# A second pair of f tiles of the first chunk by seven products, with its first loads reordered and later chunk loads on ScalarE's queue

## The chip, the cores and the metric

The kernel runs on one core of a Trainium2 chip. The metric is the device time of one execution in microseconds (us). The recorded time before is 542.76 us, the median of three runs (542.32 to 544.04). A profile covers one execution and its span is some 1.8 us shorter than the metric (540.9 us against 542.71 in the profiled run before).

In the profile PE is TensorE's matmuls, PEld its weight loads, DVE is VectorE, ACT ScalarE, POOL GpSimd and SP SyncE; a `q` behind the name means the engine's DMA queue. A bank is one of the buffers in which TensorE adds up its results. A line of the timeline gives start, length, engine, line of the kernel, operation, output and inputs, form, count, and in brackets what ended the idle time before it.

## The reference

```python
# x: 2048 x 1024, w_gate and w_up: 1024 x 3584, w_down: 3584 x 1024, all bf16
def reference(x, w_gate, w_up, w_down):
    return (_gelu(x @ w_gate) * (x @ w_up)) @ w_down
```

## The kernel before

The kernel works in two halves of 1024 tokens. In each, it goes through 28 tiles of 128 columns of f, for two blocks of 512 tokens. Two f tiles, two halves of the inner dimension and two token blocks make a 2 x 2 by 2 x 2 block product, which takes eight block products plainly, or seven by a Strassen-like scheme. `pair_quads` does the seven (M1 to M7). Its weights' sums (s1 to s4) and the sums of x (t1 to t4) are fp32r tiles; M1 and M2 multiply bf16 blocks as they were loaded. A chunk is the load of the gate and up weights of four f tiles, thus of two pairs. "Product" alone means VectorE's multiplication of gelu(gate) by up, into `hT`; a "bank addition" is VectorE adding the copy of M5 to a bank.

```python
        def do_m5(j):
            mm(V_[j], j, s(j, "s1"), tsum["t1"], True)
            m5[j] = m_pool.tile([P, TB], F32, name=f"m5_{j}")
            act(nc.scalar.copy(out=m5[j][:], in_=banks[V_[j]][:]))
            ...
        for j in range(2):                       # M7
            mm(RB[j], j, s(j, "s3"), tsum["t3"], False)
            add_m5(V_[j], RB[j])                 # VectorE, PSUM + SBUF
            ...
        for j in range(2):                       # M4: needs RB[j] free, and t4
            mm(RB[j], j, s(j, "a22"), tsum["t4"], False)
```

In the first half, the first chunk (four f tiles, two pairs) is done plainly, in eight units of 16 bf16 matmuls, while the sums are made beside it; pair 2 is the first by seven products:

```python
            first_units(hT)                      # tiles 0 and 1, first token block
            unit(hT, PB, 2, 0)
            t_sum("t1")
            unit(hT, QB, 3, 0)
            ...                                  # t2, b22, unit (0,1), t3, s sums of pair 2
            unit(hT, RB, 1, 1)
            t_sum("t4")
            unit(hT, QB, 2, 1)
            unit(hT, VB, 3, 1)
            first_pair = PPG                     # 2
```

In the later pairs of that half VectorE also makes sums of w_down ("steps", into `o_sb` buffers, stored to `t_dram`), and x of the second half is transposed into `o_sb` buffers and stored to `x_dram`.

## Time and profile before

| | before |
|---|---|
| time, median | 542.76 us |
| span of the profile | 540.9 us |
| PE busy, share of the span | 534.2 us, 99% |
| DVE, ACT, POOL busy | 360.4, 258.4, 246.0 us |
| first matmul of pair 2 | 34.19 us |

The table says that only fewer or quicker matmuls, or gaps of TensorE, can shorten this kernel. The lines behind it stand in the prediction. Busy time of TensorE is no pace: its matmuls overlap in the trace, so I read the distance of their starts.

### The profile page before, as it was taken

How to read it: one execution, taken by the hardware profiler on the slowest of the kernel's cores; microseconds unless marked ns; L12 is line 12 of the kernel's file. 1: busy time of each engine (PE TensorE's matmuls, PEld its weight loads, DVE VectorE, ACT ScalarE, POOL GpSimd, SP SyncE). 2: the span in 40 equal slices, each digit the busy share in tenths (PEclk: the TensorE clock that was granted, in tenths of full speed). 3: DMA queues.
4: the chain of work that ended last, by engine and by line, in shares of the span. 5: the costliest groups of instructions: out<-in, count | busy, mean ns of one | idle time of the engine just before them, and what ended most of it. 6: DMA issues, size and time to landing. Idle time of an engine off the chain costs nothing.

```text
span 540.9 us, 7082 instructions
## 1 busy us (share of the span) xinstructions
PE 534.2 (99%) x2356; PEld 374.8 (69%) x2392; DVE 360.4 (67%) x465; ACT 258.4 (48%) x439; POOL 246.0 (45%) x206
## 2 busy tenths in 40 slices
PE   8999999999999999999999999999999999999997
PEld 3457777766676676767776667777777766866865
DVE  0747878787886998889573433444445469969961
ACT  2435555555555319216465555555554552452270
POOL 0187888888887000000046777667777730000000
PEclk9999999999999999999999999999999999999999
DMA  9926495685837976779950405041331456677846
GB/s 221 307 80 209 125 341 161 211 256 191 277 132 227 333 240 219 266 248 311 331 196 1 155 2 155 4 153 42 114 98 59 155 204 209 228 242 247 288 148 205
DMA packets 84771, 102.70 MB, mean 190 GB/s; under 512 B 18688, under 2 KB 66304, under 8 KB 84736
## 3 DMA queue, kind: packets, MB, share of 16 engines
q1 hardware_dynamic: 83136, 101.47, 58.8%
q10 hardware_dynamic: 1600, 0.79, 0.6%
q8 instruction: 19, 0.31, 0.2%
q14 instruction: 16, 0.13, 0.1%
HBM read 85.98 MB, written 12.58 MB: 182 GB/s over the span
## 4 chain that ended last, share of the span: by engine, by line
PE 95%; DMA 3%; issue 1%; POOL 0%; ACTq 0%; DVE 0%; ACT 0%; SPq 0%
PE bank L388 58%; PE bank L658 32%; PE bank L252 5%; DMA x_dram<-o_sb 2%; DMA w_mem<-in_w_up_dram 1%; POOL s_mem L360 0%; ACTq L161 0%; DVE hT L276 0%; ACT o_sb L711 0%; ACTq L167 0%; SPq L161 0%; DVE o_sb L593 0%; ACTq L711 0%; SPq L612 0%
## 5 line engine op out<-in xcount | busy, mean ns | idle before, releaser
L388 PE MATMUL bank<-t_mem,s_mem 128*128 128x512 f32 x1016 | 240.4, 395 | 0.1
L388 PEld LDWEIGHTS bank<-t_mem,s_mem 128*128 128x128 f32 x1016 | 190.8, 188 | 42.5 <-DVE hT L276 0.5
L360 POOL TENSOR_TENSOR s_mem<-w_mem 128x512 fp32r<-128x512 bf16 x100 | 119.3, 1213 | 191.6 <-DVE t_mem L244 102.2
L658 PE MATMUL bank<-t_mem,s_mem 128*128 128x512 f32 x544 | 127.4, 393 | 0.0
L276 DVE TENSOR_TENSOR hT<-w_mem,bank 128x512 bf16<-128x512 f32 x104 | 70.6, 686 | 75.7 <-PE bank L388 42.5
L658 PEld LDWEIGHTS bank<-t_mem,s_mem 128*128 128x128 f32 x544 | 102.0, 188 | 22.5 <-issue 0.5
L411 DVE TENSOR_TENSOR bank<-bank,m 128x512 f32<-128x512 f32 x104 | 68.0, 694 | 56.2 <-ACT m L433 51.9
L388 PE MATMUL bank<-xT,w_mem 128*128 128x512 bf16 x391 | 93.0, 380 | 1.3
L271 ACT ACTIVATE w_mem<-bank 128x512 f32<-128x512 f32 x104 | 61.0, 596 | 62.3 <-DVE bank L411 39.0
L388 PEld LDWEIGHTS <-w_mem 128*128 128x128 bf16 x416 | 38.7, 98 | 49.8 <-issue 6.3
L360 POOL TENSOR_TENSOR s_mem<-w_mem,s_mem 128x512 fp32r<-128x512 bf16 x50 | 65.8, 1337 | 0.0
L568 DVE TENSOR_TENSOR t_mem<-w_mem 128x1024 fp32r<-128x1024 bf16 x56 | 65.6, 1218 | 0.0
L360 POOL TENSOR_TENSOR s_mem<-s_mem,w_mem 128x512 fp32r<-128x512 f32 x50 | 63.2, 1284 | 0.0
L438 ACT COPY bank<-bank 128x512 f32<-128x512 f32 x52 | 29.6, 570 | 38.2 <-PE bank L388 37.9
L373 ACT CAST s_mem<-w_mem 128x512 fp32r<-128x512 bf16 x52 | 32.0, 615 | 29.1 <-PE bank L388 25.4
L633 DVE TENSOR_TENSOR s_mem<-hT 128x512 fp32r<-128x512 bf16 x52 | 35.7, 714 | 10.2 <-PE bank L658 9.4
L658 PEld LDWEIGHTS <-hT 128*128 128x128 bf16 x224 | 21.3, 98 | 26.6 <-issue 2.1
L433 ACT COPY m<-bank 128x512 f32<-128x512 f32 x52 | 30.5, 587 | 17.4 <-PE bank L388 17.4
L442 ACT COPY bank<-bank 128x512 f32<-128x512 f32 x52 | 29.6, 570 | 13.8 <-PE bank L388 13.8
L711 ACT CAST o_sb<-bank 128x512 bf16<-128x512 f32 x28 | 15.3, 585 | 39.7 <-PE bank L658 39.7
L593 DVE TENSOR_TENSOR o_sb<-wd_sb,o_sb 128x512 fp32r<-128x512 bf16 x28 | 33.6, 1200 | 0.4
L252 PE MATMUL bank<-xT,w_mem 128*128 128x512 bf16 x125 | 28.0, 379 | 0.6 <-DMA w_mem<-in_w_up_dram 0.4
(42 smaller groups left out, 252.4 us busy)
## 6 DMA issues: line engine op xcount, KB each, us to landing
t_mem<-t_dram SPq DMA_DIRECT2D x56, 512.0 KB, 5.3
w_mem<-in_w_gate_dram SPq DMA_DIRECT2D x11, 1024.0 KB, 5.5
w_mem<-in_w_up_dram SPq DMA_DIRECT2D x11, 1024.0 KB, 7.9
wd_sb<-in_w_down_dram SPq DMA_DIRECT2D x28, 256.0 KB, 4.4
t_dram<-o_sb SPq DMA_DIRECT2D x28, 256.0 KB, 2.4
wd_sb<-in_w_down_dram SPq DMA_DIRECT2D x12, 512.0 KB, 8.3
w_mem<-in_w_down_dram SPq DMA_DIRECT2D x10, 512.0 KB, 6.2
w_mem<-in_w_down_dram SPq DMA_DIRECT2D x4, 1024.0 KB, 6.6
```

The lines of the kernel that those rows point to most:

```text
L252: nc.tensor.matmul(ps[:], lhsT=w_sb[:, kd, fi * P : (fi + 1) * P], rhs=xT[tb][:, kd, :], start=(kd == 0), stop=(kd == KD - 1),)
L271: act(nc.scalar.activation(out=g_sb, in_=ps[:], func=ACT.Gelu_apprx_tanh))
L276: nc.vector.tensor_tensor(out=hT[:, fc, tb * TB : (tb + 1) * TB], in0=g_sb, in1=ps[:], op=ALU.mult,)
L360: pool(nc.gpsimd.tensor_tensor(out=t, in0=in0, in1=in1, op=op))
L373: act(nc.scalar.copy(out=t, in_=a(1, 1)))
L388: nc.tensor.matmul(banks[bank][:], lhsT=lhs[:, c, :], rhs=rhs[:, c, :], start=start and c == 0, stop=c == KH - 1, skip_group_check=True,)
L411: nc.vector.tensor_tensor(out=banks[dst][:], in0=banks[src][:], in1=m5[j][:], op=ALU.add)
L433: act(nc.scalar.copy(out=m5[j][:], in_=banks[V_[j]][:]))
L568: dve(nc.vector.tensor_tensor(out=t, in0=in0, in1=in1, op=ALU.subtract))
L593: dve(nc.vector.tensor_tensor(out=t, in0=in0, in1=in1, op=ALU.subtract))
L633: dve(nc.vector.tensor_tensor(out=t, in0=in0, in1=in1, op=op))
L658: nc.tensor.matmul(banks[bset[u]][:], lhsT=lhs(i, u), rhs=rhs(i), start=start and i == 0, stop=stop and i == NS - 1, skip_group_check=True,)
```

## The change

The diff is shortened; words in square brackets stand for calls. Its intent: pair 1 (f tiles 2 and 3) by seven products too; the first loads in the order in which they are needed; and the side work of the later pairs so placed that VectorE and the loads don't get in the way.

```diff
-    for j in range(2):
-        load_xT(xT, 0, 0, KH + j, KH + j + 1)
-        load_w(first, j, 2, 5, act, 0, FA)
+    load_w(first, 0, 2, 5, act, 0, FA)
+    load_w(first, 1, 2, 5, sp, 0, FA)
...
-    for j in range(2):
-        load_w(first, j, 5, KD, sp, 0, FA)
-    for kd in range(KH + 2, KD):
+    for kd in range(KH, KD):
         load_xT(xT, 0, 0, kd, kd + 1)
+        if kd == KH + 1:
+            for j in range(2):
+                load_w(first, j, 5, KD, act, 0, FA)
...
-            unit(hT, PB, 2, 0)
-            ... (six units)
+            first_pair = PPG - 1
+            for j in range(2):
+                s_sum(0, first_pair, j, "s1")              # GpSimd
+                s_sum(0, first_pair, j, "s3")
+            s_sum(0, first_pair, 0, "s2", True)            # True: on VectorE
+            s_sum(0, first_pair, 0, "s4", True)
+            t_sum("t1")
+            pair_quads(hT, 0, first_pair, (0, PPG), {}, 0) # M1 and M2 only
+            ...
+            s_sum(0, first_pair, 1, "s2", True)
+            t_sum("t2")
+            ... (tiles 0 and 1, second token block, by halves of k; t3 between)
+            s_sum(0, first_pair, 1, "s4", True)
+            t_sum("t4", 0, KH // 2)                        # other half: after M6
...
-                        load_w(key, j, 0, KD)
+                        load_w(key, j, 0, KD, act)
...
-                then["m7"] = [store_x]
-                then["m3"] = steps[:1] + [stage loads]
-                then["m4"] = steps[1:]
+                then["m2 of last"] = [chunk load] + steps[:2] + [stage_x twice]
+                then["m7"] = [store_x] + [stage loads]
+                then["m4"] = steps[2:]
```

The rest is bank numbers, the engines that copy the first transposes of x, down sums that move from M5 to M6 in pairs 7 to 10, and GpSimd's sums for pair 2, which wait for t4.

More of the change, by code (lines that the diff above doesn't have):

```diff
@@ L224, in half, with t_sum @@
         return slice(j * KH, (j + 1) * KH)
-    def t_sum(name):
+    def t_sum(name, c0=0, c1=KH):
         def b(j, l):
@@ L243, in t_sum @@
             t2 = tsum["t2"].bitcast(F32)
-            dve(tt(out=t, in0=b(1, 0), in1=t2, op=sub))
+            cs = slice(c0, c1)
+            dve(tt(out=t[:, cs], in0=b(1, 0)[:, cs], in1=t2[:, cs], op=sub))
         else:
@@ L298, in transpose_x0 @@
         for n, (kd, ts0, ts1) in enumerate(parts):
-            tp = banks[(PB + QB)[(2 * q + n) % 4]][:].bitcast(BF16)
+            tp = banks[(VB + RB[1:])[n]][:].bitcast(BF16)
             for ts in range(ts0, ts1):
@@ L308, in transpose_x0 @@
             cols = slice(ts0 * P, ts1 * P)
-            if n % 2 == 0:
+            if q == 0 or n == 0:
                 dve(nc.vector.tensor_copy(out=xT[0][:, kd, cols], in_=tp[:, cols]))
@@ L316, in first_units @@
         wg, wu = chunks[first]
-        held = (VB, RB)
+        held = (PB, RB)
         transpose_x0(0)
-        order = [(0, 0), (0, 1), (1, 0), (1, 1)]
-        order += [(j, kd) for kd in range(2, KD) for j in range(2)]
-        for j, kd in order:
+        for kd, j in [(kd, j) for kd in range(KD) for j in range(2)]:
             for u in range(2):
@@ L337, in block, with s_sum @@
         return w_sb[:, half(kh), fi * P : (fi + 1) * P]
-    def s_sum(h, pair, j, name, on_dve=False):
+    def s_sum(h, pair, j, name, on_dve=False, ring=False):
         key = (h, "p", pair)
@@ L343, in a @@
             return block(key, j, i, kh)
-        if on_dve and name in ("s1", "s2", "s3"):
+        if ring and name in ("s1", "s2", "s3"):
             if j == 0:
@@ L378, with pair_quads @@
     pending = []
-    def pair_quads(hT, h, pair, nxt, then):
+    def pair_quads(hT, h, pair, nxt, then, part=None):
         key = (h, "p", pair)
@@ L402, in prep @@
         def prep(j, name):
-            if nxt is not None:
+            if nxt is not None and part is None:
                 s_sum(nxt[0], nxt[1], j, name)
@@ L438, in do_m6 @@
             act(nc.scalar.copy(out=banks[RB[j]][:], in_=banks[QB[j]][:]))
-        for j in range(2):
-            mm(P_[j], j, block(key, j, 0, 0), b11, True)
-            act(nc.scalar.copy(out=banks[QB[j]][:], in_=banks[P_[j]][:]))
+        if part != 1:
+            for j in range(2):
+                mm(P_[j], j, block(key, j, 0, 0), b11, True)
+                act(nc.scalar.copy(out=banks[QB[j]][:], in_=banks[P_[j]][:]))
+        if part == 0:
+            m2()
+            return
         behind = len(pending) > 0
@@ L455, in pair_quads @@
         else:
-            pending.append(m2)
+            if part is None:
+                pending.append(m2)
             order = (do_m5, 0), (do_m6, 0), (do_m6, 1), (do_m5, 1)
@@ L811 @@
             first_units(hT)
-            unit(hT, PB, 2, 0)
-            t_sum("t1")
-            unit(hT, QB, 3, 0)
-            t_sum("t2")
-            t_sum("b22")
-            unit(hT, VB, 0, 1)
-            t_sum("t3")
-            for name in S_NAMES:
-                for j in range(2):
-                    s_sum(0, PPG, j, name)
-            unit(hT, RB, 1, 1)
-            t_sum("t4")
-            unit(hT, QB, 2, 1)
-            unit(hT, VB, 3, 1)
-            first_pair = PPG
+            first_pair = PPG - 1
+            for j in range(2):
+                s_sum(0, first_pair, j, "s1")
+                s_sum(0, first_pair, j, "s3")
+            s_sum(0, first_pair, 0, "s2", True)
+            s_sum(0, first_pair, 0, "s4", True)
+            t_sum("t1")
+            pair_quads(hT, 0, first_pair, (0, PPG), {}, 0)
+            for j in range(2):
+                s_sum(0, first_pair, j, "a22")
+            t_sum("b22")
+            s_sum(0, first_pair, 1, "s2", True)
+            t_sum("t2")
+            for k0 in range(0, KD, KH):
+                for u, bset in enumerate((PB, RB)):
+                    for b, w_sb in zip(bset, chunks[first]):
+                        for kd in range(k0, k0 + KH):
+                            mm_gu(banks[b], w_sb, u, 1, kd)
+                    if k0 > 0:
+                        unit_out(hT, bset, u, 1)
+                    if k0 > 0 and u == 0:
+                        t_sum("t3")
+            s_sum(0, first_pair, 1, "s4", True)
+            t_sum("t4", 0, KH // 2)
             xs = [(tb, kd) for tb in (1, 0) for kd in range(KD)]
@@ L838, in load_chunk @@
                     for j in range(2):
-                        load_w(key, j, 0, KD)
+                        load_w(key, j, 0, KD, act)
                 if key not in chunks:
                     then["m2 of last"] = [load_chunk]
-            if h == 0:
-                n = [min(4 * (pair - first_pair + d), NSTEP) for d in range(3)]
+            if h == 0 and pair >= PPG:
+                n = [min(4 * (pair - PPG + d), NSTEP) for d in range(3)]
                 steps = [lambda k=k: stage_step(k) for k in range(n[0], n[1])]
                 new = range((n[1] + 2) // 3, (n[2] + 2) // 3)
-                then["m2 of last"] = [
-                    lambda q=q: stage_x(*q) for q in xs[:2]
-                ] + then.get("m2 of last", [])
-                then["m7"] = [store_x]
-                then["m3"] = steps[:1] + [lambda i=i: stage_load(i) for i in new]
-                then["m4"] = steps[1:]
+                then["m2 of last"] = (
+                    then.get("m2 of last", [])
+                    + steps[:2]
+                    + [lambda q=q: stage_x(*q) for q in xs[:2]]
+                )
+                then["m7"] = [store_x] + [lambda i=i: stage_load(i) for i in new]
+                then["m4"] = steps[2:]
                 xs = xs[2:]
             if pair == NPAIR - 2:
-                then["m2 of last"] = [
-                    lambda: load_wd_rows(0, 4),
-                    lambda: load_wd_rows(4, 8),
-                ]
+                then.setdefault("m2 of last", []).extend(
+                    [lambda: load_wd_rows(0, 4), lambda: load_wd_rows(4, 8)]
+                )
             if 6 < pair < 11:
                 i = 2 * pair - 8
-                then.setdefault("m5", []).append(
+                then.setdefault("m6", []).append(
                     lambda i=i: s_down(hT, 0, "s3", i, i + 2)
@@ L895, with late_t4, late_s @@
                 }
-            pair_quads(
-                hT, h, pair, (h, pair + 1) if pair + 1 < NPAIR else None, then
-            )
+            if pair < PPG and h == 0:
+                def late_t4():
+                    t_sum("t4", KH // 2, KH)
+                    last_on["t4"] = last_on["dve"]
+                def late_s():
+                    last_on["pool_wait"] = last_on["t4"]
+                    for name in S_NAMES:
+                        for j in range(2):
+                            s_sum(0, PPG, j, name)
+                then = {"m5": [late_t4], "m4": [late_s]}
+            nxt = (h, pair + 1) if pair + 1 < NPAIR else None
+            part = 1 if (h, pair) == (0, PPG - 1) else None
+            pair_quads(hT, h, pair, nxt, then, part)
         then0 = {"m5": [lambda: s_down(hT, 0, "s3", 4, 6)]}
@@ L917, in s_fill @@
                 for name in names:
-                    s_sum(nh, 0, j, name, True)
+                    s_sum(nh, 0, j, name, True, True)
             then0["m6"] = [
```

## The prediction

> **What bounds the kernel now.** I read the busy shares first, then TensorE's waits, then the chain that ended last, and only then the first 35 us as a timeline, because the change rewrites just that part and reshuffles some side work of the later pairs.
>
> The busy shares and the two matmul groups that the change trades against each other:
>
> ```profile
> PE 534.2 (99%) x2356; PEld 374.8 (69%) x2392; DVE 360.4 (67%) x465; ACT 258.4 (48%) x439; POOL 246.0 (45%) x206
> ...
> L388 PE MATMUL bank<-t_mem,s_mem 128*128 128x512 f32 x1016 | 240.4, 395 | 0.1
> ...
> L388 PE MATMUL bank<-xT,w_mem 128*128 128x512 bf16 x391 | 93.0, 380 | 1.3
> ...
> L252 PE MATMUL bank<-xT,w_mem 128*128 128x512 bf16 x125 | 28.0, 379 | 0.6 <-DMA w_mem<-in_w_up_dram 0.4
> ```
>
> TensorE is busy 99% of 540.9 us and idles next to nothing before any group. The whole wait list of TensorE has two rows, both in the first 9 us:
>
> ```profile
> PE bank L203 <- PEq L962: 0.8, 1, 0.8
> PE bank L252 <- DMA w_mem<-in_w_up_dram: 0.4, 1, 0.4
> ```
>
> So time can only come from fewer or quicker matmuls, from the start, or from gaps that this wait list hides. The chain (start, length, what) shows one such gap:
>
> ```profile
> 95.68 12.51 PE bank L388 x55
> ...
> 108.24 5.94 PE bank L388 x26
> ...
> 117.29 8.13 DMA x_dram<-o_sb
> 125.48 0.57 issue
> 126.05 0.69 DVE hT L276
> 126.74 0.04 issue
> 126.79 7.12 PE bank L388 x29
> ...
> 133.96 12.52 PE bank L388 x55
> ```
>
> Pieces that begin at the same point of a pair of f tiles lie 12.56 us apart (108.24 - 95.68). From 108.24 to 133.96 there are 25.72 us instead of 25.12, so one pair lost **0.60 us**: a VectorE step waited for a store of staged x to give back its buffer, the next hT product came late behind it, and TensorE needed its bank. Everywhere else the spacing is 12.56.
>
> The start, as a timeline (start, length, engine, what, idle before it):
>
> ```profile
> 7.28 1.05 PE L252 MATMUL bank<-xT,w_mem 128*128 128x512 bf16 x4
> ...
> 8.71 25.15 PEld L252 LDWEIGHTS <-w_mem 128*128 128x128 bf16 x118 [0.87 <-DMA w_mem<-in_w_up_dram]
> 8.71 25.64 PE L252 MATMUL bank<-xT,w_mem 128*128 128x512 bf16 x115 [0.38 <-DMA w_mem<-in_w_up_dram]
> ...
> 20.67 2.18 ACT L247 CAST t_mem<-xT 128x512 fp32r<-128x512 bf16 x4 [1.23 <-DMA xT<-in_x_dram]
> ...
> 34.19 1.89 PE L388 MATMUL bank<-xT,w_mem 128*128 128x512 bf16 x8
> ```
>
> The reader is to see that from 8.71 on, TensorE runs unbroken up to the first pair by seven products at about 34.1, and that the last x of the second token block is in place only at 20.67, where ScalarE's conversion stopped waiting for it.
>
> **What the Trainium skill says.** "Perfetto Trace Analysis", section "Identifying the Most-Contended Engine", says that matmul busy time is a poor measure of headroom. This trace agrees: one matmul is listed at 380 ns, but 118 of them start over 25.64 - 0.38 = 25.26 us, thus 25.26/117 = **0.216 us** apart. "TensorE: Matmul & The Clock Gate", section "Back-to-back issue gap", gives N/2.4 + 2.5 ns for a warm matmul, 215.8 ns at N = 512; the trace has 216. No page gives the fp32r pace; I take it from the pair: 56 matmuls in 12.56 us, of which 16 bf16 take 3.45, so 40 fp32r take 9.11, or **0.228 us** each. "SBUF — State Buffer", section "Who interferes with whom", says a VectorE instruction with two SBUF inputs and a GpSimd one that reads SBUF exclude each other. The trace agrees: two GpSimd sums from 27.97 took 4.32 us together beside t3 and t4 (1.15 each alone), and t4 took 3.02 against 2.28 us for t1 to t3. "DMA: Bandwidth & Descriptors", section "Issuing engines are not separate DMA queues", says that loads issued on several engines share the same 16 DMA engines, so another queue saves issue time only. The two-microsecond windows give DMA shares of 0.98 to 1.29 from 2 to 18 us at 218 to 291 GB/s, so the start is already near what they move, and moving loads to ScalarE's queue cannot make the data come much sooner.
>
> **The change, part by part.**
> 1. *Matmuls.* Before, the first chunk is eight plain units of 16 bf16 matmuls. After, four of them (tiles 2 and 3, both token blocks, 64 matmuls, 64 x 0.216 = 13.8 us) become seven products: 16 bf16 and 40 fp32r, 12.56 us. On the path, since TensorE is the bound: **-1.25 us** (13.81 - 12.56). Seven for eight would be 12.5%, but the fp32r pace gives part of it back and one pair out of 28 is concerned.
> 2. *First loads.* The up weights of k 2 to 4 were fourth on ScalarE's queue (issued 2.38, landed 8.7) and now go out third on SyncE, at some 1.8, ahead of both x transposes. TensorE's order becomes k by k. TensorE stood without weights for 0.32 us at 7.70 and 0.87 us at 8.71. I expect the larger gap to shrink by about 0.6. The matmuls would then reach k = 4 near 9.5 instead of 10, for which the transpose, now issued half a microsecond later, is just in time. First gain, by estimate: **-0.5 us**. Ten matmuls were done at 8.71; in the new order eight should be done by about 7.8.
> 3. *New sums.* Pair 1 needs ten left sums of its own (s1 to s4 and a copy, for gate and up); those on GpSimd cost 1.15 us each, those on VectorE 0.69. They stand where GpSimd was idle (it waited 22.22 us for its first sum). VectorE has four more bank additions and the t sums must all come some 8 us sooner. Off the path if they are in time; part 4 asks.
> 4. *Deadlines.* From k = 2 at 7.8: 24 matmuls finish the first units at 13.0; M1 and M2 of pair 1 end at 16.4 (16 x 0.216); the second token block's first half is then needed, and its second half 16 matmuls later, at 19.9. Those units end at 23.3, and 40 fp32r matmuls bring the end of pair 1 to 32.4. Before, the same point was at 34.1, so the ideal gain is 1.7 us, parts 1 and 2 together. But the last x was there at 20.67 before. It goes out perhaps 1 us sooner, behind the same bytes on busy engines; I put it at 20.0 to 20.5, a wait of up to 0.5. Then VectorE has one chain from it: t2 2.28, product 0.69, t3 2.28, product 0.69, half of t4 1.14, two bank additions 1.40, the other half 1.14, one addition 0.69, together 10.3 us, ending at about 30.5 to 31, with GpSimd able to stretch a t sum by 0.7. M4 needs that bank at 30.7 in the ideal line. So I give back **+0.7 us** for x and this chain. Next, GpSimd's sums for pair 2 wait for t4: s1 twice and s2 twice are done 4 x 1.2 = 4.8 us after about 31, while M6 of pair 2 asks for s2 some 2.6 us after 33, so that is just met.
> 5. *Later pairs.* Two steps move to where the last M2 ends, chunk loads go to ScalarE, and x transposes come after them. The store that held the buffer at 117.29 is no longer behind a 2 MB chunk load on the same queue. I count most of the 0.60 us gap as gone: **-0.45 us**. ScalarE pays two issues of about 0.6 us every second pair; it has 48% load, and its next copy waits for M6 anyway, so nothing on the path.
>
> Sum: -1.25 - 0.5 + 0.7 - 0.45 = -1.5 us; 542.76 - 1.5 = 541.3 us.
>
> **The rivals.**
> (a) *The wait only moves*: the second block of x or the up weights of tiles 2 and 3 are late, because the second half of the chunk is now asked for at 13.0 (gate) and 13.9 (up) instead of 13.5 and 15.2, and the start is set by bytes. For it: the DMA shares above 1 up to 18 us, and the conversion that waited until 20.67. Against: those loads are issued a microsecond sooner. Then the start gains nothing and only the gap at 126 is saved: about 542.3 us, or 543 if GpSimd stretches the t sums too.
> (b) *Everything hidden*: the x is there by 19.9 and VectorE keeps up. Then -1.25 - 0.5 - 0.6 = -2.35, or 540.4 us.
> (c) *A new bound in the later pairs*: VectorE has two steps (0.7 to 1.3 us each) between the last M2's product and the bank additions, plus a 0.7 us down sum in pairs 7 to 10. The old trace has about 2.8 us there (112.0 to 114.83) and M3 can wait some 1 us more, so 3.4 fits, without much to spare. If it doesn't fit, each of a dozen pairs could lose 0.1 to 0.3: 543 to 544 us.
>
> **Range and chances.** Rival (b) sets the low end, 540.0 with noise; (a), or a mild (c), the high end, 542.9. The three runs before spread over 1.7 us, as much as the whole effect. A change of 2% is 10.9 us: no term here comes near, so within 2% has 0.98; I leave 0.01 for each side.
>
> **What would show it.** 64 matmuls of the plain group (L252) left instead of 128, 40 more fp32r and 16 more bf16 ones by quads; the weight wait before the third k of at most 0.3 us; the first matmul of pair 2 at about 33.1 us (34.1 before: ideal 32.4); TensorE waits between 16 and 32 us on x, on VectorE's t sums or on bank additions, together some 0.7 us; spacing of 12.56 us in all later pairs and no loss near 126. I am wrong if the pairs' spacing grows, if pair 2 starts later than 34.1, or if TensorE's wait list shows GpSimd sums.

## The result

The changed kernel takes 541.69 us (median of six runs, 541.14 to 544.24); the kernel before, run with it, 543.1 (542.32 to 544.08). The ratio is 0.9978, with a 95% interval of 0.9955 to 1.0. Ratios here are the mean time of one kernel's runs over that of the other's of the same rounds, so not quite the ratio of the medians. In a second session the changed kernel gave 541.22 (541.14 to 541.54) against 542.65, a ratio of 0.9976 [0.9961, 0.9991]. All clocks are 0.999 or 1.0. So the change brings 1.2 to 1.4 us, or 0.2%; that is far inside the 2% within which two kernels count as the same.

The page of the changed kernel, its busy shares and the same groups:

```profile
PE 534.5 (99%) x2384; PEld 377.1 (70%) x2384; DVE 362.2 (67%) x475; ACT 263.3 (49%) x446; POOL 239.5 (44%) x210
...
L389 PE MATMUL bank<-t_mem,s_mem 128*128 128x512 f32 x1056 | 249.7, 394 | 0.2 <-DVE bank L412 0.2
...
L389 PE MATMUL bank<-xT,w_mem 128*128 128x512 bf16 x432 | 98.1, 380 | 0.2 <-DMA w_mem<-in_w_up_dram 0.2
```

There are 40 more fp32r matmuls (1056 against 1016) and 16 more bf16 ones by quads (432; the weight loads before were 416), as the trade wants. TensorE now waits for VectorE's bank additions (L412) and for up weights. Three of the six rows of its wait list (waiter, waited for, us in total, times, longest; the others are 0.8 us at the very start, 0.2 for x and 0.2 for up weights):

```profile
...
PE bank L253 <- DVE xT L312: 0.2, 1, 0.2
PE bank L389 <- DVE bank L412: 0.2, 1, 0.2
PE bank L389 <- DMA w_mem<-in_w_up_dram: 0.2, 1, 0.2
...
```

The chain that ended last shows more than those small numbers. It no longer runs over TensorE in the first 32 us but over the transposed loads of x and then VectorE (start, length, what):

```profile
14.22 4.28 DMA xT<-in_x_dram
...
27.12 0.60 DVE s_mem L358
27.72 0.83 DVE t_mem L245
28.55 0.23 issue
28.78 1.28 DVE bank L412 x2
30.06 1.12 DVE t_mem L245
31.19 0.62 DVE bank L412
31.81 0.04 issue
31.85 152.82 PE bank L389 x680
```

From 31.85 us TensorE runs 152.82 us without a break, through the place near 126 us where the kernel before lost 0.60. Before 31.85, VectorE's sums and bank additions set the start of M4. The step from x to VectorE in this chain is no wait, though: VectorE was at t1 until 20.31 (17.07 + 3.24). The timeline of that start, first VectorE's, then GpSimd's and ScalarE's, then TensorE's rows:

```profile
14.69 0.91 DVE L358 TENSOR_TENSOR s_mem<-s_mem,w_mem 128x512 fp32r<-128x512 f32 x1
15.63 1.52 DVE L358 TENSOR_TENSOR s_mem<-w_mem,s_mem 128x512 fp32r<-128x512 bf16 x1
17.07 3.24 DVE L236 TENSOR_TENSOR t_mem<-xT,xT 128x2048 fp32r<-128x2048 bf16 x1
20.24 0.68 DVE L277 TENSOR_TENSOR hT<-w_mem,bank 128x512 bf16<-128x512 f32 x1
20.84 0.68 DVE L358 TENSOR_TENSOR s_mem<-s_mem,w_mem 128x512 fp32r<-128x512 f32 x1
21.44 2.28 DVE L239 TENSOR_TENSOR t_mem<-xT,t_mem 128x2048 fp32r<-128x2048 bf16 x1
...
12.78 5.38 POOL L360 TENSOR_TENSOR s_mem<-w_mem 128x512 fp32r<-128x512 bf16 x4 [11.48 <-DMA w_mem<-in_w_gate_dram]
...
18.52 2.18 ACT L248 CAST t_mem<-xT 128x512 fp32r<-128x512 bf16 x4 [0.43 <-DMA xT<-in_x_dram]
...
14.54 2.76 PE L389 MATMUL bank<-xT,w_mem 128*128 128x512 bf16 x12 [0.21 <-DMA w_mem<-in_w_up_dram]
17.14 7.07 PE L253 MATMUL bank<-xT,w_mem 128*128 128x512 bf16 x32
23.86 7.78 PE L389 MATMUL bank<-t_mem,s_mem 128*128 128x512 f32 x32
31.85 2.10 PE L389 MATMUL bank<-t_mem,s_mem 128*128 128x512 f32 x8 [0.21 <-DVE bank L412]
33.80 1.90 PE L389 MATMUL bank<-xT,w_mem 128*128 128x512 bf16 x8
```

From 13.48 on, VectorE has no idle time until the bank additions before M4 (31.85). M4's eight matmuls are the row at 31.85, pair 2 begins at 33.80. It began at 34.19 before: the start gives 0.39 us. The rest of the 1.2 us between the spans (540.9 and 539.7) is the 0.60 near 126 us, and 0.2 in the down stage, where the profile before had a few small delays put down to "issue" that none of the others repeats in full; I make nothing of those.

### The profile page after: what moved, and what is told of

Same layout as the page of the kernel before. It is cut to its first block, busy times and chain, and to the rows that moved or that the text cites. A ratio compares the mean times of both kernels' runs of the same rounds, so it can differ in the third digit from the quotient of the medians.

```text
span 539.7 us, 7117 instructions
## 1 busy us (share of the span) xinstructions
PE 534.5 (99%) x2384; PEld 377.1 (70%) x2384; DVE 362.2 (67%) x475; ACT 263.3 (49%) x446; POOL 239.5 (44%) x210
## 4 chain that ended last, share of the span: by engine, by line
PE 93%; SPq 2%; DVE 1%; issue 1%; DMA 1%; ACT 0%; ACTq 0%; DVEq 0%
PE bank L389 61%; PE bank L664 33%; SPq L172 2%; DMA xT<-in_x_dram 1%; SPq L161 0%; DVE hT L277 0%; DVE t_mem L245 0%; DVE bank L412 0%; DVE s_mem L358 0%; DVE t_mem L239 0%; ACT o_sb L717 0%; SPq L167 0%; ACTq L717 0%; DVEq L239 0%
## 5 line engine op out<-in xcount | busy, mean ns | idle before, releaser
L389 PE MATMUL bank<-t_mem,s_mem 128*128 128x512 f32 x1056 | 249.7, 394 | 0.2 <-DVE bank L412 0.2
L389 PEld LDWEIGHTS bank<-t_mem,s_mem 128*128 128x128 f32 x1056 | 198.2, 188 | 44.3 <-DVE bank L412 0.9
L360 POOL TENSOR_TENSOR s_mem<-w_mem 128x512 fp32r<-128x512 bf16 x104 | 121.9, 1195 | 196.8 <-DVE t_mem L245 116.2
L664 PE MATMUL bank<-t_mem,s_mem 128*128 128x512 f32 x544 | 127.2, 392 | 0.0
L664 PEld LDWEIGHTS bank<-t_mem,s_mem 128*128 128x128 f32 x544 | 102.1, 188 | 22.2
L412 DVE TENSOR_TENSOR bank<-bank,m 128x512 f32<-128x512 f32 x108 | 69.8, 693 | 44.9 <-ACT m L434 42.7
L389 PE MATMUL bank<-xT,w_mem 128*128 128x512 bf16 x432 | 98.1, 380 | 0.2 <-DMA w_mem<-in_w_up_dram 0.2
L360 POOL TENSOR_TENSOR s_mem<-w_mem,s_mem 128x512 fp32r<-128x512 bf16 x50 | 62.2, 1268 | 0.0
L360 POOL TENSOR_TENSOR s_mem<-s_mem,w_mem 128x512 fp32r<-128x512 f32 x50 | 58.0, 1180 | 0.0
L439 ACT COPY bank<-bank 128x512 f32<-128x512 f32 x54 | 30.8, 570 | 39.0 <-PE bank L389 38.5
L639 DVE TENSOR_TENSOR s_mem<-hT 128x512 fp32r<-128x512 bf16 x52 | 34.2, 685 | 10.2 <-PE bank L664 9.4
L444 ACT COPY bank<-bank 128x512 f32<-128x512 f32 x54 | 30.8, 570 | 12.8 <-PE bank L389 12.8
L599 DVE TENSOR_TENSOR o_sb<-wd_sb,o_sb 128x512 fp32r<-128x512 bf16 x28 | 31.4, 1121 | 0.5
L571 ACT CAST t_mem<-w_mem 128x1024 fp32r<-128x1024 bf16 x28 | 26.9, 1047 | 0.0
```

The lines of the kernel that those rows point to most:

```text
L360: pool(nc.gpsimd.tensor_tensor(out=t, in0=in0, in1=in1, op=op))
L389: nc.tensor.matmul(banks[bank][:], lhsT=lhs[:, c, :], rhs=rhs[:, c, :], start=start and c == 0, stop=c == KH - 1, skip_group_check=True,)
L412: nc.vector.tensor_tensor(out=banks[dst][:], in0=banks[src][:], in1=m5[j][:], op=ALU.add)
L439: act(nc.scalar.copy(out=banks[RB[j]][:], in_=banks[QB[j]][:]))
L599: dve(nc.vector.tensor_tensor(out=t, in0=in0, in1=in1, op=ALU.subtract))
L639: dve(nc.vector.tensor_tensor(out=t, in0=in0, in1=in1, op=op))
```

## The experiments

All these kernels gave correct results and were run beside the kernel before, on the same chip. Effects are some tenths of a us, and single times scatter by more, so the verdicts rest on three landmarks of the traces: **A**, the first real matmul; **T**, the start of t1 on VectorE; **B**, the first matmul of pair 2. A moves with the landing of the first x (5.27 to 6.00 us over all traces). In start_only, its repeat and best2 the first four matmuls take 1.42, 1.45 and 1.69 us instead of 1.02, so their B - A holds up to 0.67 us of that; B - T doesn't.

| kernel | time, median us | ratio [95%] | A | B | B - A | B - T | lost near 126 |
|---|---|---|---|---|---|---|---|
| before | 542.76 | - | 5.54 | 34.19 | 28.65 | - | 0.60 |
| changed | 541.69 | 0.9978 [0.9955, 1.0] | 5.38 | 33.80 | 28.42 | 16.73 | 0 |
| after_again | 541.22 | 0.9976 [0.9961, 0.9991] | 5.35 | 33.52 | 28.17 | 16.72 | 0 |
| later_only | 542.46 | 1.0001 [0.9988, 1.0014] | 5.57 | 34.57 | 29.00 | - | 0 |
| start_only | 546.74 | 1.0053 [1.002, 1.0085] | 5.77 | 33.77 | 28.00 | 15.76 | 0.46 |
| start_only_again | 542.0 (one run) | - | 5.48 | 33.68 | 28.20 | 16.72 | 0.47 |
| queue_only | 541.92 | 0.998 [0.9966, 0.9994] | 6.00 | 34.81 | 28.81 | - | 0 |
| steps_only | 541.9 | 0.9979 [0.9966, 0.9993] | 5.41 | 33.63 | 28.22 | - | 0 |
| plain_pair1 | 541.94 | 0.9986 [0.9974, 0.9998] | 5.55 | 33.62 | 28.07 | - | 0 |
| plain_again | 541.55 | 0.9983 [0.9966, 1.0] | 5.50 | 33.57 | 28.07 | - | 0 |
| extra_sum | 542.12 | 0.999 [0.9978, 1.0002] | 5.71 | 34.26 | 28.55 | 17.44 | 0 |
| pool_j1 | 540.95 | 0.9963 [0.995, 0.9977] | 5.27 | 32.91 | 27.64 | 16.27 | 0 |
| best1 | 541.55 | 0.9973 [0.996, 0.9985] | 5.45 | 33.33 | 27.88 | 16.07 | 0 |
| best2 | 545.44 | 1.003 [0.9998, 1.0062] | 5.36 | 33.79 | 28.43 | 16.26 | 0 |

The loss is the distance between the M1 starts of two pairs near 120 and 133 us, less 12.56.

My theory after the result: the change has two halves that act apart, and in the first half the seven products don't pay, because VectorE takes as long for its sums and additions as the trade saves on TensorE. Rivals: the seven products bring it all; or x and weights, not VectorE, bound the start.

### The later pairs alone

```diff
# kernel before, only:
-                        load_w(key, j, 0, KD)
+                        load_w(key, j, 0, KD, act)
# and m2 of last / m7 / m3 / m4 / m6 lists as in the change
```

> The kernel before with only the later-pair part of the change (chunk loads on ScalarE's queue, two steps earlier, stage loads earlier, down sums at M6). Theory (the change's gain has two separate halves): the start is as before, pair 2's first matmul at 34.2 us, and the 0.60 us loss between 108 and 134 us is gone, so a span of about 540.3 us against 540.9, ratio 0.9985 to 0.999. Rival (the whole gain comes from the seven products): nothing changes, span 540.9, ratio 1.000.

```profile
108.21 3.63 PE L388 MATMUL bank<-xT,w_mem 128*128 128x512 bf16 x16
...
120.77 3.63 PE L388 MATMUL bank<-xT,w_mem 128*128 128x512 bf16 x16
...
133.33 2.98 PE L388 MATMUL bank<-xT,w_mem 128*128 128x512 bf16 x13
```

The M1 starts of three pairs, by TensorE's timeline of this run, are 12.56 us apart twice: the loss is gone, with the old start. So that half of the gain doesn't come from the seven products. The times show nothing (1.0001). In the profiled run the start was a slow one, B at 34.57, 0.38 later than in the first profile of the same start; whether that holds for the other four runs is not known. My expected 34.2 was a miss by that much; the old start waits for its weights, and those move from run to run (34.19, 34.57, 34.81, 33.63 in four traces).

### The new start alone

```diff
# changed kernel, only: the later-pair lists and the chunk loads' queue put back
-                        load_w(key, j, 0, KD, act)
+                        load_w(key, j, 0, KD)
```

> The changed kernel with its later pairs put back as before. Theory: pair 2's first matmul at 33.8 us as in the changed kernel, and the 0.60 us loss in one pair (steps that wait for the store of staged x) is back, so a span of about 540.4 us (539.7 + 0.6). Rival (the loss near 126 us was a coincidence of timing of the old start, or is removed by the new start): no such loss, span 539.7.

```profile
125.02 0.69 DVE L599 TENSOR_TENSOR o_sb<-wd_sb 128x512 fp32r<-128x512 bf16 x1 [1.24 <-DMA x_dram<-o_sb]
```

VectorE's timeline shows the wait of before again (1.24 us for the store of staged x, 1.37 before), and the pair loses 0.46 us. The theory holds here. But the six times are 542.04, 542.62 and four from 546.72 to 547.88. By the rule of 1.5% all count, so the ratio of 1.0053 mixes two kinds of runs and can't be used.

> The new start with the old later pairs once more, for a profile of the slow one of its two times (four runs of six took 546.7 to 547.9 us, two 542.0 to 542.6). If the slow one is caught: the 5 us are in pairs 2 to 13 of the first half, as waits of VectorE on buffers or of TensorE on GpSimd's sums, because only there does this kernel differ from the changed one. Rival: the lost time is spread over the whole span with a lower clock.

It caught a quick run (542.0) with the same loss of 0.47 us. What makes some executions 5 us longer stays open; it shows again below in one other variant, and no trace has caught it.

### The queue, or the order of the steps

```diff
# queue_only: kernel before, only
-                        load_w(key, j, 0, KD)
+                        load_w(key, j, 0, KD, act)
# steps_only: kernel before with the later-pair lists of the change, chunk loads still on SyncE
```

> The kernel before with nothing changed but the queue of the later chunk loads (ScalarE's for SyncE's). Theory (the store of staged x lands late because a 2 MB chunk load is issued just ahead of it on SyncE, at 116 us): the chunk load goes out at the last M2, some 5 us earlier, the store lands sooner, and the 0.60 us loss between 108 and 134 us shrinks to under 0.2. Rival (the order of VectorE's steps makes the wait): the loss stays at 0.5 to 0.6 us. Times about 0.5 us apart, too close for the rounds; the trace decides.

> The kernel before with the later pairs' steps, stage loads, staged x and down sums in the changed order, the chunk loads still on SyncE's queue. Theory (queue): the loss of 0.60 us between 108 and 134 us stays at 0.4 or more. Rival (order of the steps, and of the buffers they take): the loss is gone, and the queue is not needed for it.

Neither loses anything near 126 us: either alone is enough, so my theory was too narrow. The timelines of SyncE and ScalarE say what they share. Before, the gate chunk load went out at 116.11, the up chunk load at 116.73, and the store of x right behind, at 117.29; it landed 8.13 us later. With queue_only the chunk loads go out at 111.29 and 113.15, with steps_only at 111.73 and 112.28, in the changed kernel at 110.29 and 111.14. So in all three the chunk load goes out 3.6 to 5.8 us earlier, ahead of the transposes of x. The store then goes out later than before (122.61 and 121.45), behind transposes that take longer to land (median 6.1 and 4.4 us, 2.8 before), but its own median time to landing falls from 5.0 to 2.2 and 2.3 us. VectorE's wait before the step in question, before and in queue_only:

```profile
125.44 0.69 DVE L593 TENSOR_TENSOR o_sb<-wd_sb 128x512 fp32r<-128x512 bf16 x1 [1.37 <-DMA x_dram<-o_sb]
...
124.85 1.43 DVE L593 TENSOR_TENSOR o_sb<-wd_sb 128x512 fp32r<-128x512 bf16 x1 [0.15 <-DMA x_dram<-o_sb]
```

In steps_only no wait on that store is left. In the changed kernel VectorE still waits 1.11 us for it, in later_only 0.98, but there the product behind it comes in time. What counted for TensorE was not the wait but how late that product began: 5.7 us after the pair's M1 in the kernel before, 5.2 in queue_only, 4.1 in the changed kernel. The intervals of both times lie below 1 (0.998 and 0.9979), but the profiled run of steps_only also had the quickest of the old starts.

### Tiles 2 and 3 as plain units again

```diff
# changed kernel, only:
-            first_pair = PPG - 1
-            ... (sums, pair_quads for pair 1)
+            unit(hT, VB, 2, 0)
+            t_sum("t1")
+            unit(hT, QB, 3, 0)
+            ... (t2, b22, unit (0,1), t3, s sums of pair 2)
+            unit(hT, RB, 1, 1)
+            t_sum("t4")
+            unit(hT, QB, 2, 1)
+            unit(hT, VB, 3, 1)
+            first_pair = PPG
```

> The changed kernel with tiles 2 and 3 as four plain units again (64 bf16 matmuls in place of 16 bf16 and 40 fp32r), its loads, its order by k and its later pairs kept. Theory (most of the 1.25 us that the trade is worth on TensorE is eaten by a wait for the up weights of tiles 2 and 3, 0.4 us, and by VectorE's additions, 0.7 us): from 13.3 us on, 96 matmuls at 0.216 us run unbroken, pair 2 starts at about 34.0 us against 33.8, span about 539.9. Rival (the trade pays in full): pair 2 starts at 35.0 us, span 540.9.

> The changed kernel with four plain units for tiles 2 and 3, once more. Theory (the new loads let 128 plain matmuls run unbroken): 28.0 to 28.2 us from the first real matmul to pair 2's first one, as before; the 0.5 us wait for a reload of t2 in the last down stage may come again. Rival (the unbroken start was luck, as it also came once with the old loads): a wait for weights, 28.4 us or more.

```profile
6.86 26.93 PE L253 MATMUL bank<-xT,w_mem 128*128 128x512 bf16 x124
33.62 1.89 PE L389 MATMUL bank<-xT,w_mem 128*128 128x512 bf16 x8
```

TensorE's timeline of plain_pair1: after its first four matmuls the other 124 run unbroken, and pair 2 starts at 33.62 (33.57 the second time), where the changed kernel has 33.80 and 33.52. The two pairs of traces don't differ: **eight units of plain matmuls reach pair 2 as soon as the seven products do.** My theory expected 34.0 and so was too kind to the seven products: it counted from a start that had already lost time on weights.

So the gain of the start, as far as it stands out of the runs' own scatter, comes from the new loads and the order by k that goes with them; no run tells these two apart. Counted from the first real matmul, plain units with the new loads took 28.07 us twice, with the old loads 28.65, 29.00, 28.81 and 28.22. In plain_pair1's profile a wait of 0.5 us for a reload of t2 in the last down stage cost that run its gain again; the second profile of the same kernel has none. The medians are 541.22 for the changed kernel and 541.55 for the plain one, with overlapping ranges.

### One more sum on VectorE

```diff
             s_sum(0, first_pair, 1, "s4", True)
+            s_sum(0, first_pair, 1, "s4", True)
             t_sum("t4", 0, KH // 2)
```

> The changed kernel with the last VectorE sum of pair 1 (s4 of the up weights, 0.69 us) done twice. Theory (VectorE's chain of sums and bank additions sets when M4 of pair 1 may start): M4 starts 0.6 to 0.7 us later than 31.85, pair 2 at about 34.45 us, span 540.3. Rival (the late x or GpSimd sets it, VectorE has slack): pair 2 still at 33.8 us, span 539.7.

```profile
26.78 1.41 DVE L358 TENSOR_TENSOR s_mem<-w_mem,s_mem 128x512 fp32r<-128x512 bf16 x2
...
32.31 2.11 PE L389 MATMUL bank<-t_mem,s_mem 128*128 128x512 f32 x8 [0.22 <-DVE bank L412]
```

VectorE makes the sum twice (1.41 us for two), and M4, TensorE's row here, starts at 32.31 instead of 31.85. Counted from t1, which by chance started 0.25 us sooner here, pair 2 comes 0.71 us later (17.44 against 16.73): the whole added sum. VectorE's work is what M4 waits for. start_only seems to differ (B - T is 15.76), but doesn't: its t1 started at 18.01, after GpSimd's first four sums (over at 17.54), and took 2.28 us; in the changed kernel it started at 17.07 beside them (over at 18.16) and took 3.24. Both end at 20.3, and from the end of t1 to pair 2 it is 13.48 and 13.49 us, in the two repeats 13.47 and 13.48, with the added sum 14.20.

The traces also show what sets the start of VectorE's chain. GpSimd's four sums begin when the gate weights of tiles 2 and 3 have landed: at 12.78 us in the changed kernel, after 11.48 us of waiting for that load. From there to pair 2 it is 21.02 us in the changed kernel, in after_again and in start_only_again, 21.17 in start_only, and 21.74 with the added sum. The 0.25 us that t1 started sooner in extra_sum is the 0.26 by which these weights came sooner. So it was not x that bounded the start but, by these distances, the landing of these weights, through GpSimd and VectorE. No run moved this load alone, so this is read from the traces and not tested.

### Two sums to GpSimd

```diff
-            s_sum(0, first_pair, 1, "s2", True)
+            s_sum(0, first_pair, 1, "s2")
...
-            s_sum(0, first_pair, 1, "s4", True)
+            s_sum(0, first_pair, 1, "s4")
```

> The changed kernel with the two sums of pair 1 for the up weights (s2 and s4, 0.69 us each on VectorE, on its chain between 20 and 28 us) moved to GpSimd, which stands idle from 18.2 to 31.4 us there. Theory (VectorE's throughput from 14.7 to 31.8 us sets the start of M4): M4 starts 0.5 to 1.3 us sooner than 31.85 (0.5 if GpSimd's sums lengthen the t sums beside them), pair 2 at 32.6 to 33.3 us. Rival (the two engines exclude each other, so a 1.15 us sum on GpSimd costs VectorE as much as it saves): pair 2 at 33.7 to 34.0 us.

```profile
20.40 2.65 DVE L239 TENSOR_TENSOR t_mem<-xT,t_mem 128x2048 fp32r<-128x2048 bf16 x1
20.98 3.10 POOL L360 TENSOR_TENSOR s_mem<-w_mem,s_mem 128x512 fp32r<-128x512 bf16 x1
...
32.91 1.90 PE L389 MATMUL bank<-xT,w_mem 128*128 128x512 bf16 x7
```

Pair 2 starts at 32.91, 0.89 us sooner than in the first profile of the change. Of that, t1 started 0.43 sooner (16.64 against 17.07), as the gate weights of tiles 2 and 3 did (GpSimd began at 12.35 against 12.78), which is the run's own luck; B - T falls by 0.46, from 16.73 to 16.27. A sum holds VectorE's next instruction back by 0.60 us (20.84 to 21.44), so two sums taken away are 1.20 us; but t2 and t3 took 2.65 us each instead of 2.28, which gives 0.74 of it back and leaves 0.46, as measured. Each of them began while one of GpSimd's sums was still running: t2 at 20.40, with a sum that ended at 20.90, t3 at 23.57, with one that ended at 24.08. Both theories had a part of it. This is the quickest kernel: 540.95 us, 0.9963 [0.995, 0.9977] of the kernel before. Its interval overlaps those of the changed kernel, so that it is quicker than that one rests on the traces.

### Further steps on top of it

best1 adds to pool_j1:

```diff
-                load_w(first, j, 5, KD, act, 0, FA)
+                load_w(first, j, 5, KD, (act, sp)[j], 0, FA)
...
-                then = {"m5": [late_t4], "m4": [late_s]}
+                then = {"m7 first": [late_t4], "m4": [late_s]}   # after M7's first addition
```

> pool_j1, and the second half of t4 taken after the first bank addition of M7 instead of before it (1.14 us later in VectorE's order, since M4's first two matmuls need only the first half of t4), and the up weights of k 5 to 7 issued on SyncE instead of behind a wait on ScalarE's queue. Theory: M4 is bound by TensorE, not by VectorE, pair 2 starts at 32.5 to 32.9 us, span about 538.8 us, ratio to before 0.996. Rival (x or weights arrive too late for that): pair 2 at 33.3 us or later, with waits on loads in TensorE's list.

```profile
14.71 2.76 PE L389 MATMUL bank<-xT,w_mem 128*128 128x512 bf16 x12 [0.73 <-DMA w_mem<-in_w_up_dram]
```

A miss. B - T shrinks a little more (16.07), but the load moved to SyncE holds back the loads behind it (up weights of tiles 2 and 3 issued at 8.84 instead of 8.08), and TensorE waits 0.73 us for the up weights of tiles 2 and 3, so B is 33.33. Pair 2 itself then takes 11.19 us to pair 3's M1 (44.52 - 33.33) where the changed kernel takes 10.83 (44.63 - 33.80). GpSimd's sums for pair 2 start behind the late half of t4, at 31.65 against 30.43 in pool_j1, and pair 2's weight loads wait for them twice (0.25 us at 40.52, 0.36 at 41.65); in pool_j1 there is no such wait.

best2 adds to pool_j1:

```diff
-        load_w(first, j, 0, KD, sp, FA, FG)
+        load_w(first, j, 0, KH, sp, FA, FG)
...                                              # behind the last copy of x0 on ScalarE:
+                for i in range(2):
+                    load_w(first, i, KH, KD, act, FA, FG)
```

> pool_j1 with the second pair's weights loaded by halves of k, the first halves on SyncE, the second on ScalarE's queue after the last copy of x. M1 needs only the first half. Theory (in pool_j1 a wait of 0.4 us for the up weights comes before VectorE's chain can bind): the wait is gone, and from the first real matmul to pair 2's takes 27.3 to 27.6 us against 27.64. Rival (VectorE's chain alone binds): 27.6 to 27.8 us, the wait moved to M4. Or the x of the second block comes later by two more issues: over 27.8.

M1 and M2 run without a wait, as meant (13.38 to 16.84 us), but M4 waits for VectorE again and B is 33.79. The first four matmuls started some 0.42 us apart here, as far as the eight matmuls on constants with which the kernel begins and twice the usual (why is not known), so the second transposes came at 6.89 instead of 6.13 us, and t1 in turn at 17.53. B - T is pool_j1's to 0.01. Its times are 541.85 and 541.92 beside four from 544.74 to 550.67 (the longest, over 1.5% above the fastest, counts as slow and is not in the ratio); like start_only it has quick and long runs. A kernel with such runs is no improvement, whatever its best one.

A repeat of the changed kernel:

> The changed kernel once more, to see how much its start moves from run to run. From the first real matmul to pair 2's first one it took 28.42 us in its first profile. Theory (seven products cost VectorE's chain what they save on TensorE): 28.0 to 28.5 us again, so no clear gain over plain units' 28.07. Rival (the first profile was an unlucky one, the trade does pay): 27.3 us or less.

B - A is 28.17, within the theory's range, and B - T is 16.72, the first profile's to 0.01.

## Why the prediction was right

The time was foretold at 541.3, within 540.0 to 542.9, and came out at 541.69. The sum was right to 0.4 us; not all of its terms were, so the closeness of the total is in part luck.

**Matmuls (-1.25).** The counts came as said, 64 plain ones gone and 40 and 16 added, and in steady pairs the pace is the same 12.56 us for 56. As TensorE work the saving is there. As time it isn't: against the same kernel with plain units, pair 2 starts no sooner.

**First loads (-0.5).** About right, but the term can only be given roughly: 28.07 us from the first real matmul with the new loads and plain units, 28.22 to 29.00 with the old ones, which is 0.15 to 0.93 less. The reasoning that the start is near what the DMA engines move, so that data cannot come much sooner, did not hold: the last x was there at 18.52 instead of 20.67, and the same view of the old start has 352 to 366 GB/s from 20 to 26 us.

**Deadlines (+0.7).** This is the step that failed. "VectorE has one chain from it: t2 2.28, product 0.69, t3 2.28, ..., together 10.3 us" let the chain begin with the last x, put at 20.0 to 20.5. In the trace x was there at 18.52, where ScalarE's conversion stopped waiting, and TensorE did not wait for it; but t2 began only at 21.44, since VectorE was still busy with what lies ahead of it: three sums of pair 1 (14.69, 15.63 and 20.84) and t1, of which the first two sums and t1 took 0.91, 1.52 and 3.24 us beside GpSimd's four sums instead of 0.68, 0.68 and 2.28. The chain's length was about right, 10.4 us from t2 to M4: one more sum, which I had left out (27.04), is made up by instructions that overlap. So the chain isn't bound by x; it begins with the gate weights of tiles 2 and 3 and GpSimd's sums, and VectorE is busy throughout, 18.48 of the 20 us from 12 to 32. M4 comes at 31.85 instead of 30.7, and pair 2 at 33.80 and 33.52 where I had 33.1, and 32.4 without any wait. The term is 1.1 to 1.4 us, not 0.7, and with it the seven products break even.

On TensorE the loss lies in two places: 0.7 us before M4 (the 40 fp32r matmuls take 9.94 and 9.96 us to pair 2, against 9.28 in pair 2 itself), and 0.4 to 0.7 us at the up weights of tiles 2 and 3, which is rival (a): M1 and M2 take 3.84 and 4.14 us instead of 3.45. The two don't simply add: start_only did not wait for these weights, lost 0.8 us before M4, and reached pair 2 no sooner.

**Later pairs (-0.45).** The gap gave all of its 0.60. The mechanism (a store right behind a chunk load) fits the three traces, which have the chunk load earlier in common, though the queue isn't needed for it: the order of the steps alone does it too. Rival (c), a new bound in those pairs, didn't come: they are 12.56 us apart. ScalarE's issues cost nothing on the path.

Terms too small and too large offset each other: the start and the gap gave 0.99 us in the traces, of 1.5 foretold, the small delays that only the first profile had another 0.2, and the times say 1.2 to 1.4. The range held since it was built from the rivals, not from the sum alone.

## What to carry to other kernels

Work saved on the bound engine is time only where the engines that feed it keep up: before trading matmuls for sums, add up everything the summing engine has to do up to the product that needs the last sum, not only the chain from the last load, and ask which load that work begins with. Measure such a trade against the same kernel without it, from a landmark inside the trace; here the total had improved by other parts of the same change. And look at what a small store that frees a buffer is issued behind: right behind a large load it cost 0.60 us here.

## What the Trainium skill lacked or had wrong

- "TensorE: Matmul & The Clock Gate", section "Back-to-back issue gap", also gives some 131 ns for a sustained stream of 512-column matmuls, each with its weight load. This kernel's unbroken streams run at 216 ns (124 bf16 matmuls in 26.93 us), which its isolated-matmul formula fits. The fp32r pace, 228 ns by the spacing of pairs, is on no page.
- No page speaks of executions of one program on one core that fall into two groups at almost the same clock (542 and 547 us in start_only, 542 and 545 to 551 in best2, at mean clocks of 0.996 to 1.0). No trace here caught a long one.
